# Four small edits to a fused attention and MLP kernel: the first load in two transfers, a longer row of constant products, another order of the three products of the second layer, and the weighted values at the end of a step

## The chip, the cores and the metric

The kernel runs on one core of one Trainium2 chip. The metric is the device time of one launch in microseconds (us); smaller is better. The core's engines are TensorE (PE in the rows, its weight loads PEld), VectorE (DVE), ScalarE (ACT), GpSimd (POOL) and SyncE (SP, which here issues nearly all DMA transfers). Each engine works through its own queue in order.

## The reference

Banded attention with a few global columns, then an MLP over all tokens:

```
q, k, v: (4, 8, 768, 64) fp32; n_global = 8; n_local = 96
scores = q k^T / 8 - slope_h * distance, kept where column < n_global or 0 <= row - column < n_local
a = softmax(scores);  attn = a v                       -> x, (3072, 512)
h = x @ w_in          (512 -> 2048)
g = h * clip(h + 3, 0, 6) / 6
out = g @ w_out       (2048 -> 512), fp32
```

The weights arrive as 64-bit words and are decoded to fp32 on the chip.

## The kernel before, in words

Tokens are worked in 8 blocks of 384 (two for each of 4 batch elements). A block's attention has 4 pairs of heads. The first three blocks (pairs 0 to 11) are attended ahead of everything else, in the loop of `banded` over `n` from -2 to 12; the later blocks' attention is woven into the MLP of the block before them (`attention`). The weights are decoded on DVE, ACT and POOL in between (`decode`, four steps for each of 32 chunks), at a pace that `work` sets from given costs.

Step `n` of the early loop does, in program order: the distances of pair n+2 (`distances`, ACT and POOL, n up to 1); `scores(t)` of pair n+2 for its three row tiles (PE, line 773); then for t = 0, 1, 2: `weigh` of pair n+2 (DVE line 788 adds the distances and takes the row's least value, ACT line 792 takes the exponential and the sums), `turn(t)` of pair n (PE transposes, lines 818 and 820, copied out by ACT or, for t = 1, DVE, line 822), and at t = 0 `sum_up` (DVE lines 800 and 801), at t = 1 `normalize` (POOL line 810) of pair n+1. `values` of pair n-1 stands at t = 1: PE products (line 862) into the only bank of the pool `xp`, then `put_x`: `xh` by ACT (line 152) and `xl` by DVE (line 153). It ends with the load of later values on SP. While `self.more` holds (n up to 7) the banks of the MLP serve as score banks and no half of the MLP is worked; from n = 8 the halves of the first MLP block go in between.

The order of PE, SP and POOL is the program's, pinned by `in_order`. The order on DVE and ACT is chosen by the framework's scheduler when the kernel is built.

At the start `banded_setup` issues `iv` (four integers, broadcast to 128 partitions) on ACT's queue and the loads of pairs 0 and 1 on SP's (`load`, line 289: 504 columns of keys and 384 of queries, 888 fp32 columns in one transfer). The masks are built from `iv`, from them `distances`, and the first `weigh` needs these. `wake` (line 353) issues seven products of a constant on PE, each two instructions, ahead of the first scores.

The MLP works in units of f (16 for each block): `first` (12 products of 384 columns, line 166), `gate` and the split of the gate's result into a high part `gh` (ACT or POOL) and a low part `gl` (DVE line 191, from `gh`), and `second` (line 198), nine products of 512 columns: for each of three row tiles gh x w2h, gl x w2h, gh x w2l. `second` of one f stands behind `first` of the next.

Of the kernel before, what the change touches and what calls it, by code (L numbers as in the profile page):

```python
# [21 lines left out]
TB = NT * P  # L22
# [10 lines left out]
KW = PREV + NT * TG  # L33
QW = 2 * TB
VW = 2 * NT * P
LOAD = KW + QW + VW
# [8 lines left out]
BOTH = 10  # L45
ROOMS = 2
MORE = 3
LEAD = 6
WAKE = 7
FIRST = 6  # L50

def store(nc, pool, out, row, acc, last=False):
# [6 lines left out]
class Kernel:  # L59
# [134 lines left out]
    def second(self, f, acc, gh, gl):  # L194
        for tt in range(NT):
            tk = slice(tt * P, (tt + 1) * P)
            for j, (a, w) in enumerate(((gh, self.w2h), (gl, self.w2h), (gh, self.w2l))):
                self.nc.tensor.matmul(acc[tt], lhsT=a[:, tk], rhs=self.w2(w, f),  # L198
                                      start=(f == 0 and j == 0), stop=(f == NF - 1 and j == 2))

# [84 lines left out]
    def load(self, n, values):  # L285

        if n < len(self.blocks) * NPAIR:
            columns = slice(KW + QW, LOAD) if values else slice(0, KW + (TB if n < BOTH else QW))
            self.nc.sync.dma_start(out=self.place(n)[:, columns], in_=self.pairs[n, :, columns])

    def load_next(self, n, values):

# [55 lines left out]
    def wake(self):  # L348

        any_ = self.three.broadcast_to([P, P])  # L350
        out = self.ps_x.tile([P, BANK], F32, name="xp")[:, 0:P]
        for _ in range(WAKE):
            self.nc.tensor.matmul(out, lhsT=any_, rhs=any_, start=True, stop=True)
# [99 lines left out]
    def banded(self, flag):  # L453

        self.banded_setup()
        start = len(self.nc.cur_bb.bb.instructions)
        self.common(2, 2)
        self.ps_s = self.pool("ps_s", 1, PSUM)
        self.ps_t = self.pool("ps_t", 1, PSUM)
        self.ps_x = self.pool("ps_x", 1, PSUM)  # L460
        self.turn, self.more, self.score_banks = {}, True, 1
        self.wake()
        self.raw, self.z, self.e, self.given, self.decoded = {}, {}, {}, [0.0, 0.0], 0
        self.last, self.op = None, None
        self.weights()
        with ExitStack() as early, ExitStack() as words:
            x0 = self.x_tiles(self.pool("x0", 1, ctx=early, side="right"))
            xs = [x0, self.x_tiles(), self.x_tiles()]
            self.decoding(words, 2, 2, side="right")
            self.decoding_steps = self.decode()  # L470

            def decoded_all():
                words.close()
                self.op = self.pool("op", 2, ctx=early, side="right")

            self.decoded_all = decoded_all
            self.fetch(0)
            self.given[1] = LEAD
            self.allowed = 4 * NF + 3
            acc = []  # L480
            with ExitStack() as ctx:
                self.room += self.rooms(self.pool("more", 1, ctx=ctx), MORE - ROOMS, ROOMS)
                self.load(2, False)
                self.fetch(1)
                for n in range(ROOMS):
                    self.load(n, True)
                self.plain_distances(ctx)
                self.attending(ctx, 0, 9, 5)
                pairs = [Pair(self, n, xs[n // NPAIR], True) for n in range(EARLY)]
                todo = self.halves([(0, f, xs[0], acc) for f in range(FIRST)])  # L490

                def half():
                    if not self.more:
                        next(todo, None)

                for n in range(-2, EARLY + 1):
                    if n + 2 < NPAIR:
                        self.distances(n + 2)
                    if n == 8:
                        self.more = False  # L500
                        acc.extend(self.acc_tiles())
                    if n + 2 < BOTH:
                        weigh = [pairs[n + 2].scores(t) for t in range(NT)]
                        self.load_next(n + 2, False)
                        self.work(1.440, 0)
                    for t in range(NT):
                        if n + 2 < EARLY:
                            if n + 2 < BOTH:
                                weigh[t]()
                            else:  # L510
                                pairs[n + 2].scores(t)()
                                if t == NT - 1:
                                    self.load_next(n + 2, False)
                            self.work(0 if n + 2 < BOTH else 0.78, 0.64)
                            if t == NT - 1 and n == -2:
                                self.load(2, True)
                        if 0 <= n < EARLY:
                            pairs[n].turn(t)
                            self.work(0.396, 0)
                        if n + 1 in (0, 1):  # L520
                            pairs[n + 1].sum_up(t)
                            pairs[n + 1].normalize(t)
                        if t == 0:
                            if 2 <= n + 1 < EARLY:
                                pairs[n + 1].sum_up()
                            half()
                        if t == 1:
                            if n > 0:
                                pairs[n - 1].values()
                                self.work(1.350, 0.47)  # L530
                            if 2 <= n + 1 < EARLY:
                                for u in range(NT):
                                    pairs[n + 1].normalize(u)
                        if t == 2:
                            half()
                for _ in todo:
                    pass
            self.weights()
            self.allowed = 4 * (2 * NF + 1)
            acc1 = [pool.tile([P, BANK], F32, name=name) for pool, name in ((self.ps_s, "sp"), (self.ps_t, "tp"), (self.ps_x, "xp"))]  # L540
            self.given[1] = max(self.given)
            todo = [(1, f, xs[1], acc1) for f in range(FIRST)]
            todo += [(i, f, xs[i], (acc, acc1)[i]) for f in range(FIRST, NF) for i in range(2)]
            for _ in self.halves(todo):
                pass
        self.attending(self.ctx, 2, 3, 2, side="right")
        self.bp = self.pool("bp", 2, side="right")
        self.there = self.pool("there", 2, bass.MemoryType.DRAM)
        self.score_banks = 2
        self.op = self.pool("op", 3, side="right")  # L550
        x, ahead = xs[2], None
        for i in range(2, len(self.blocks)):
            units, x_next = [], None
            if i + 1 < len(self.blocks):
                x_next = self.x_tiles()
                units, ahead = self.attention(i + 1, x_next, ahead)
                if i == 2:
                    units = [[]] + units
            else:
                units = [[]] * 4 + [[lambda: self.doubt(flag)]]  # L560
            acc = self.acc_tiles()
            for k, _ in enumerate(self.halves([(i, f, x, acc) for f in range(NF)], True)):
                for unit in units[k] if k < len(units) else ():
                    unit()
            x = x_next
        self.finish()
        self.in_order(start)
        return acc
# [373 lines left out]
```

## Time and profile before

| | |
|---|---|
| time, median of 3 runs | 672.31 us (672.19 to 672.88) |
| time of the profiled execution | 671.4 us |
| its span, first to last instruction | 669.6 us |
| busy share of the span | PE 98%, PEld 87%, DVE 63%, ACT 42%, POOL 33% |

The profile is of one execution. The 1.8 us between its time and its span lie around the program. Busy PE is not PE at its best rate, so the shares are read stage by stage.

### The profile page before, as it was taken

To read this page: it belongs to the slowest core of one execution; us is meant where nothing else is said; L and a number is where in the kernel's file an instruction comes from. 1 tells how busy PE (TensorE), PEld (TensorE's weight loads), DVE (VectorE), ACT (ScalarE), POOL (GpSimd) and SP (SyncE) were. 2 spreads that over 40 slices of the span, in tenths; PEclk is the share of its full clock that TensorE was granted. 3 is DMA by queue.
4 is the path that set the end of the run, shared out by engine and by line. 5 is a ranking of instruction groups with operands and counts; after the bars stand their busy time and mean duration, and the time that the engine had idled before them with its cause. 6 is when DMAs were issued, how large, how long until landed. Compare 5 with 4: busy or idle time off the path is not lost.

```text
span 669.6 us, 11375 instructions
## 1 busy us (share of the span) xinstructions
PE 654.7 (98%) x3919; PEld 584.1 (87%) x3919; DVE 424.3 (63%) x1121; ACT 278.4 (42%) x736; POOL 217.9 (33%) x389
## 2 busy tenths in 40 slices
PE   7989999999999999999999999999999999999996
PEld 5768789888999999999999989899999999989995
DVE  6799999999235776366663876457662777422221
ACT  6798755655235333153424433143331444121111
POOL 3766621221000553133340444225340444312110
PEclk9999999999999999999999999999999999999999
DMA  8577544442004366625663366524554256510001
GB/s 294 147 233 238 176 155 150 129 155 95 1 0 134 95 173 180 181 75 135 165 163 125 88 170 185 151 83 127 147 161 134 79 150 145 139 48 1 1 1 52
DMA packets 60692, 84.73 MB, mean 127 GB/s; under 512 B 8400, under 2 KB 45264, under 8 KB 60624
## 3 DMA queue, kind: packets, MB, share of 16 engines
q1 hardware_dynamic: 60336, 83.64, 43.3%
q8 instruction: 33, 0.54, 0.3%
q14 instruction: 35, 0.29, 0.1%
q10 hardware_dynamic: 288, 0.26, 0.1%
HBM read 62.92 MB, written 20.97 MB: 125 GB/s over the span
## 4 chain that ended last, share of the span: by engine, by line
PE 81%; DVE 7%; ACT 4%; DMA 3%; POOL 2%; issue 2%; POOLq 0%; ACTq 0%; SPq 0%; DVEq 0%
PE hp L166 36%; PE acc L198 33%; ACT n L792 3%; DMA wst<-w 2%; PE sp L777 2%; PE xp L862 2%; PE tp L862 2%; PE tp L777 2%; POOL n L810 1%; DVE wz L394 1%; DVE wz L400 1%; PE sp L198 1%; PE tp L198 1%; PE xp L198 1%; DVE wz L385 1%
## 5 line engine op out<-in xcount | busy, mean ns | idle before, releaser
L177 ACT ACTIVATE g<-hp,small 128x384 f32<-128x384 f32 x127 | 73.7, 580 | 254.2 <-PE hp L166 227.5
L166 PE MATMUL hp<-xh,w1h 128*128 128x384 f32 x512 | 174.0, 340 | 0.3 <-ACT w1h L404 0.3
L166 PE MATMUL hp<-xh,w1l 128*128 128x384 f32 x512 | 172.9, 338 | 0.1
L166 PE MATMUL hp<-xl,w1h 128*128 128x384 f32 x512 | 171.9, 336 | 0.0
L184 POOL TENSOR_SCALAR gh<-g 128x384 fp32r<-128x384 f32 x96 | 51.5, 537 | 294.0 <-DVE g L178 276.8
L198 PE MATMUL acc<-w2h,gl 128*128 128x512 f32 x336 | 133.1, 396 | 0.1
L198 PE MATMUL acc<-w2l,gh 128*128 128x512 f32 x336 | 132.7, 395 | 0.0
L198 PE MATMUL acc<-w2h,gh 128*128 128x512 f32 x336 | 132.2, 393 | 0.0
L178 DVE SCALAR_TENSOR_TENSOR g<-g,hp 128x384 f32<-128x384 f32 x128 | 69.7, 545 | 86.6 <-ACT g L177 86.0
L810 POOL TENSOR_SCALAR n<-n,sums 128x232 f32<-128x232 f32 (+1 forms) x186 | 102.0, 564 | 36.6 <-DVE sums L801 17.5
L191 DVE TENSOR_TENSOR gl<-g,gh 128x384 fp32r<-128x384 f32 x128 | 79.4, 621 | 50.4 <-POOL gh L184 45.4
L792 ACT ACTIVATE n<-n,least 128x232 f32<-128x232 f32 (+1 forms) x192 | 89.0, 465 | 45.7 <-DVE least L788 44.3
L166 PEld LDWEIGHTS hp<-xh,w1h 128*128 128x128 f32 x512 | 96.3, 188 | 5.9 <-issue 1.4
L166 PEld LDWEIGHTS hp<-xl,w1h 128*128 128x128 f32 x512 | 96.2, 188 | 3.8
L166 PEld LDWEIGHTS hp<-xh,w1l 128*128 128x128 f32 x512 | 96.0, 188 | 0.4 <-DVE w1l L391 0.4
L198 PEld LDWEIGHTS acc<-w2l,gh 128*128 128x128 f32 x336 | 63.0, 188 | 13.2
L198 PEld LDWEIGHTS acc<-w2h,gl 128*128 128x128 f32 x336 | 63.2, 188 | 12.4 <-DVE gl L191 1.7
L198 PEld LDWEIGHTS acc<-w2h,gh 128*128 128x128 f32 x336 | 63.3, 188 | 10.6 <-POOL gh L184 0.3
L835 DVE STREAM_TRANSPOSE blocks<-n 128x256 f32<-128x256 f32 x112 | 43.5, 424 | 29.2 <-POOL n L810 18.7
L367 POOL TENSOR_SCALAR we<-wst 128x512 int32<-128x512 uint32 x32 | 25.5, 797 | 70.3 <-DMA wst<-w 63.2
L748 POOL TENSOR_SCALAR kx<-load 64x504 fp32r<-64x504 f32 (+1 forms) x40 | 31.1, 778 | 37.8 <-PE hp L166 36.2
L788 DVE CUSTOM_DVE_ANT_0 n<-sp,d 128x232 f32<-128x232 f32 (+1 forms) x70 | 23.7, 375 | 30.9 <-PE sp L777 30.6
(110 smaller groups left out, 780.7 us busy)
## 6 DMA issues: line engine op xcount, KB each, us to landing
wst<-w SPq DMA_DIRECT2D x32, 512.0 KB, 3.5
load<-pairs SPq DMA_DIRECT2D x22, 636.0 KB, 5.2
there<-blocks SPq DMA_DIRECT2D x52, 256.0 KB, 2.6
load<-pairs SPq DMA_DIRECT2D x32, 384.0 KB, 4.0
weights<-there SPq DMA_DIRECT2D x48, 192.0 KB, 4.1
out<-o SPq DMA_DIRECT2D x23, 256.0 KB, 2.2
weights<-there SPq DMA_DIRECT2D x32, 160.0 KB, 3.2
load<-pairs SPq DMA_DIRECT2D x10, 444.0 KB, 4.0
```

The costliest lines, as they stand in the source:

```text
L166: self.nc.tensor.matmul(hp, lhsT=self.w1(w, f)[:, kt, :], rhs=a[:, kt, :], start=(n == 0), stop=(n == 3 * NKT - 1))
L177: nc.scalar.activation(out=g, in_=hp, func=AF.Relu, bias=self.three, scale=1.0)
L178: nc.vector.scalar_tensor_tensor(out=g, in0=g, scalar=6.0, in1=hp, op0=ALU.min, op1=ALU.mult)
L184: self.nc.gpsimd.tensor_scalar(out=gh, in0=g, scalar1=1.0, scalar2=0.0, op0=ALU.mult, op1=ALU.add)
L191: self.nc.vector.tensor_tensor(out=gl, in0=g, in1=gh.bitcast(F32), op=ALU.subtract)
L198: self.nc.tensor.matmul(acc[tt], lhsT=a[:, tk], rhs=self.w2(w, f), start=(f == 0 and j == 0), stop=(f == NF - 1 and j == 2))
L748: nc.gpsimd.tensor_scalar(out=part["kx"][own, c], in0=k[own, c], scalar1=1.0, scalar2=0.0, op0=ALU.mult, op1=ALU.add)
L777: nc.tensor.matmul(sp[j][:, lo:W], lhsT=q[:, t], rhs=part["kx"][:, c], start=(m == 0), stop=(m == 1))
L792: nc.scalar.activation(out=e[:, j, lo:W], in_=e[:, j, lo:W], func=AF.Exp, bias=self.least[:, i:i + 1], scale=-1.0, accum_out=self.sums[:, ...
L810: nc.gpsimd.tensor_scalar(out=e[:, j, lo:W], in0=e[:, j, lo:W], scalar1=over, scalar2=0.0, op0=ALU.mult, op1=ALU.add)
L835: nc.vector.transpose(out=blocks[:, :, s].rearrange("p b j q -> p j b q"), in_=e[:, :, c:c + P].rearrange("p j (b q) -> p j b q", b=4))
L862: nc.tensor.matmul(xps[j * D:(j + 1) * D, t * P:(t + 1) * P], lhsT=vt[0:K, t, j * D:(j + 1) * D], rhs=self.part(t, j, c, K), start=(c == 0 ...
```

## The change

Four edits. `load` of pair 0's keys and queries becomes two transfers (keys, then queries). `wake` issues nine products and not seven. In `second` the product with `gl` is the last of each three. In the early loop, for n = 1 to 7, `values` of pair n-1 and the `work` call behind it move from t = 1 (ahead of `normalize` of pair n+1, and of `weigh` and `turn` of t = 2) to t = 2, behind `turn(2)` and so straight ahead of the next step's scores; from n = 8 they stay where they were.

```diff
-WAKE = 7
+WAKE = 9
...
-            for j, (a, w) in enumerate(((gh, self.w2h), (gl, self.w2h), (gh, self.w2l))):
+            for j, (a, w) in enumerate(((gh, self.w2h), (gh, self.w2l), (gl, self.w2h))):
...
-            columns = slice(KW + QW, LOAD) if values else slice(0, KW + (TB if n < BOTH else QW))
-            self.nc.sync.dma_start(out=self.place(n)[:, columns], in_=self.pairs[n, :, columns])
+            end = KW + (TB if n < BOTH else QW)
+            for columns in (slice(KW + QW, LOAD),) if values else (slice(0, KW), slice(KW, end)) if n == 0 else (slice(0, end),):
+                self.nc.sync.dma_start(out=self.place(n)[:, columns], in_=self.pairs[n, :, columns])
...
                         if t == 1:
-                            if n > 0:
+                            if n > 0 and not self.more:
                                 pairs[n - 1].values()
                                 self.work(1.350, 0.47)
                             if 2 <= n + 1 < EARLY:
                                 for u in range(NT):
                                     pairs[n + 1].normalize(u)
                         if t == 2:
+                            if n > 0 and self.more:
+                                pairs[n - 1].values()
+                                self.work(1.350, 0.47)
                             half()
```

## Rows read from the trace of the kernel before

**Rows 1.** Busy time by stretch: PE, PEld, DVE, ACT, POOL, granted clock, DMA share, GB/s.

```profile
10.00:15.00 5.00, 4.37 (x19) 2.74 (x15) 5.00 (x33) 5.00 (x23) 0.00 (x0) 1.00 0.96 352
...
20.00:30.00 10.00, 9.39 (x94) 7.31 (x94) 7.09 (x33) 8.04 (x30) 7.12 (x19) 1.00 0.69 176
...
120.00:170.00 50.00, 49.77 (x247) 44.25 (x247) 47.53 (x88) 27.76 (x48) 9.15 (x12) 1.00 0.36 117
170.00:270.00 100.00, 100.00 (x556) 90.78 (x556) 56.68 (x146) 37.64 (x97) 26.36 (x47) 1.00 0.36 103
```

**Rows 2.** The chain of waits, shares of the span by engine.

```profile
PE 81%; DVE 7%; ACT 4%; DMA 3%; POOL 2%; issue 2%; POOLq 0%; ACTq 0%; SPq 0%; DVEq 0%
```

**Rows 3.** The chain in order of time, first 18 us: start, us, what.

```profile
0.73 4.32 DMA iv<-bounds
...
6.83 0.60 ACT p L317 x2
...
9.32 2.65 ACT n L792 x12
...
17.29 1.20 POOL n L810 x2
```

**Rows 4.** DMA issues at 0.7 us, and the stores of the run: us to landing.

```profile
load<-pairs SPq DMA_DIRECT2D x1, 444.0 KB, 4.1
iv<-bounds ACTq DMA_DIRECT2D x1, 2.0 KB, 4.3
...
out<-o SPq DMA_DIRECT2D x23, 256.0 KB, 2.2
```

**Rows 5.** Timeline, start: start, us, instruction, [idle before <- what ended it].

```profile
0.92 3.36 PE L353 MATMUL xp<-small 128*128 128x128 f32 x14 [0.92 <-DVE small L103]
...
4.93 0.58 PE L773 MATMUL sp<-load 64*128 64x128 f32 x1 [0.65 <-DMA load<-pairs]
...
7.45 0.29 DVE L788 CUSTOM_DVE_ANT_0 n<-sp,p 128x128 f32<-128x128 f32 x1 [0.72 <-ACT p L317]
```

**Rows 6.** PE's transposes by line, 5 to 20 us, then 21 to 50 us.

```profile
L818 PE MATMUL hp<-ident,n 128*128 128x128 f32 x4 | 1.8, 448 | 1.2 <-DVE n L808 1.2
...
L818 PE MATMUL hp<-ident,n 128*128 128x128 f32 x25 | 6.5, 286 | 0.0
```

**Rows 7.** Timeline of one early step, 25 to 32 us.

```profile
25.07 2.47 POOL L810 TENSOR_SCALAR n<-n,sums 128x128 f32<-128x128 f32 x6 [0.44 <-DVE sums L801]
...
28.96 0.17 DVE L800 TENSOR_SCALAR sums<-sums 128x6 f32<-128x6 f32 x1 [1.14 <-ACT n L792]
...
29.32 0.56 DVE L153 TENSOR_TENSOR xl<-xp,xh 128x384 fp32r<-128x384 f32 x1
...
29.94 1.32 PE L862 MATMUL xp<-pt,load 128*64 128x128 f32 x20 [0.49 <-DVE xl L153]
...
30.23 0.49 ACT L792 ACTIVATE n<-n,least 128x232 f32<-128x232 f32 x1 [0.46 <-DVE least L788]
...
31.19 0.33 PE L818 MATMUL hp<-ident,n 128*128 128x128 f32 x1
```

**Rows 8.** Waits of ACT, 20 to 50 us: total, times, longest.

```profile
ACT n L792 <- DVE least L788: 3.9, 4, 2.5
```

**Rows 9.** Timeline: a low part awaited at 156 us, and the last unit.

```profile
156.24 0.19 PEld L198 LDWEIGHTS sp<-w2h,gl 128*128 128x128 f32 x1 [0.32 <-DVE gl L191]
...
661.72 0.56 DVE L191 TENSOR_TENSOR gl<-g,gh 128x384 fp32r<-128x384 f32 x1 [0.73 <-POOL gh L184]
661.74 0.51 PE L198 MATMUL acc<-w2h,gh 128*128 128x512 f32 x1
...
662.34 0.50 PE L198 MATMUL acc<-w2h,gl 128*128 128x512 f32 x1
...
662.90 0.39 PE L198 MATMUL acc<-w2h,gh 128*128 128x512 f32 x1
663.13 0.39 PE L198 MATMUL acc<-w2h,gl 128*128 128x512 f32 x1
```

## Prediction

> **What bounds the kernel now.** I read the table by stretch first. At 170 to 270 us PE is busy for all of the 100 us, and before that, at 120 to 170 us, it has 49.77 of 50 while DVE has 47.53 of 50 [rows 1]. The reader is to see two regimes: a long end that only PE sets, and a beginning in which PE is never what is short. There, at 10 to 15 us, ACT and DVE are both busy for all of the 5 us, and at 20 to 30 us the busiest engine is idle in name only: PE shows 9.39 of 10, but with small products, and ACT 8.04 [rows 1]. The chain of waits agrees: 81% of the span is PE, and the rest is the early DVE, ACT, DMA and POOL work [rows 2]. Followed in order of time, the chain starts at none of the big loads: it starts with `iv`, a transfer of 2 KB that takes 4.32 us, goes through the masks to ACT's distances at 6.83 us, runs through ACT's exponentials and reaches POOL's normalization at 17.29 us [rows 3]. PE has no part in these 17 us. So three things can move the end: the head of that chain, the ACT and DVE work of the early steps (a us won there is a us at the end, as every queue behind it moves along in its fixed order), and PE's own idle time behind.
>
> **The first load in two.** The load removed lands 4.1 us after its issue at 0.73 us, at 4.83 us; the first score product starts at 4.93 us and ends at 5.51 us [rows 3 to 5]. The DVE instruction that reads it starts at 7.45 us and waited for ACT's distances, not for PE [rows 5]. The scores have 7.45 - 5.51 = 1.94 us to spare, so earlier keys are worth nothing by themselves, and a second issue on SP, which moves every later load of the beginning back by one issue, is covered by the same 1.94 us for pair 0. What is not covered is `iv`. Its 2 KB need 4.3 us, while a store of 256 KB needs 2.2 us [rows 4]: 2.1 us of it are, by the nearest row, time beside the loads. A row of the load is 888 x 4 = 3,552 bytes and becomes 2,016, then 1,536. If the pieces of `iv` take turns with rows of the load, the 2.1 us shrink by at most 1 - 2016/3552 = 43%, or 0.9 us. At the other end nothing changes, or one more transfer stands in the way; I set that end at 0.4 us lost. As pair 1's load follows with whole rows, I take a third of the 0.9: **0.3 us won**, at the head of the chain, so in full.
>
> **Nine products for seven.** Fourteen instructions take 3.36 us, 0.24 each [rows 5]. Four more run from about 4.28 to 5.24 us and so push the first score product from 4.93 to 5.24 us at most: 0.3 of the 1.94 us to spare. Cost **0**, cover the wait for the distances; it would cost from 1.94 us on. PE then has no gap from 0.92 us through the first scores. [...]
>
> **The low part last.** In the last unit DVE starts `gl` at 661.72 us, PE's first product runs at 661.74, and the second, which needs `gl`, starts at 662.34; later ones follow each other every 0.23 us (662.90, 663.13) [rows 9]. With the product of `gh` and `w2l` second, two of the nine are issued before `gl` comes and seven, not eight, behind it: **0.23 us won**, with the store behind it moving along. The same at 156 us, where the weight load waited 0.32 us for `gl` [rows 9]: what follows is one product shorter, 0.23 us. In the stage with PE at 100% [rows 1] `gl` is early and nothing changes. The other end is that `w2l`, the last result of a chunk's decoding, is now needed 0.23 us sooner; no row shows a wait for it, so I set the loss between 0 and 0.23 and take 0. Together **0.46 us**.
>
> **The weighted values at a step's end.** For seven steps, 20 or 24 PE products, ACT's `xh`, DVE's `xl`, a load on SP and the decode steps that `work` draws move behind `normalize`, `weigh` and `turn` of t = 2. What stands ahead of the next scores on PE is the same work in both orders, the values and four transposes; only their order differs. The values wait for the `xl` before (0.49 us at 29.94), and the transposes of `turn(2)` stand behind them at 31.19 us, though POOL had finished their input at 27.54 us [rows 7]. Turned round, the transposes fill that wait, and the values have their `xl` long before. SP's load of later values is issued perhaps 1.3 us later, one length of the values [rows 7], for a pair used three steps on; a fetch of weights queued behind it would be as late, but `work` stays behind `values`, so it isn't queued differently. PE is not the bound here, though: DVE waited 1.14 us for ACT's last exponential, then did the sums and `xl`, and only then `weigh`, for which ACT waited 0.46 us [rows 7]. Such waits are 3.9 us in four times; the longest, 2.5 us, I put to the distances at the beginning, which leaves **1.4 us** in three [rows 8]. That is the most that this edit can win directly. It wins it if `xl` (0.56 us) comes out from between the sums and `weigh`. But DVE's and ACT's order is set by the scheduler from the changed program, and it may as well put `xl` where it waits longer: seven steps with another 0.46 us each lose **3.2 us**. I take half of the gain, **0.7 us**, since PE's wait for `xl` goes in any case and nothing new stands ahead of `weigh`.
>
> **The sum.** 0.3 + 0 + 0.46 + 0.7 = 1.46 us. Against the profiled execution, 671.4 us for a span of 669.6, that is 669.9; the median shown is 0.9 us above that execution, so 672.31 - 1.46 = 670.85, say **670.8 us**. 0.2%, or 1.34 us, is about what a measurement of this kernel can tell from no change; the forecast is only just beyond it.
>
> **Rivals.** *Only the ends pay*: the scheduler leaves DVE and ACT as they were, the freed PE time is idle time, and 0.3 + 0.46 remain: 671.5 us. For it: PE isn't on the early chain [rows 3]. Against: the 1.4 us of [rows 8] lie behind an instruction that moves. *The moved `xl` holds `weigh`*: 672.31 - 0.76 + 3.2 = 674.7 us, slower. It decides once a step's added wait exceeds 0.76/7 = 0.11 us. For it: `xh` now comes a step's end later, right when `weigh` of the next pair is due; against: PE has the values' inputs earlier. *The second transfer lands late*: if the queries came a whole landing time (4.1 us) after the first part, 4.1 - 1.94 = 2.2 us are lost, and 672.31 - 0.46 - 0.7 + 2.2 = 673.3 us. Against it: both parts are on the same queue, one issue apart. [...]
>
> **How the numbers follow.** Forecast 0.45, only the ends 0.31, `xl` holds `weigh` 0.16, second transfer late 0.03, clock pays 0.05. Faster by over 0.2%: 0.45 + 0.05 = 0.50. Within: 0.31 + 0.03 = 0.34. Slower: 0.16. The likeliest case's own range is 669.5 to 671.0. The range reaches from all gains at their bounds, 672.31 - 0.9 - 0.46 - 1.4 - 0.65 = 668.9, to the late second transfer, 673.4; it leaves out the slower case and a little below, under 0.2.
>
> **What would show it.** Right: `iv` lands before 5.05 us and `weigh` starts before 7.45; the last unit issues two products ahead of the wait for `gl`; ACT's waits for the least values at 25 to 50 us shrink and everything behind 50 us stands over 1 us earlier. Wrong: `iv` as late as before, or `weigh` waiting for PE; exponentials further apart than before; a wait for `w2l`; or a fetch of weights that comes later and holds the decoding, so that a gain at 50 us is gone at 170.

## The result, and the profile after

The changed kernel takes 673.5 us in the median of 20 executions (671.2 to 676.5), the kernel before beside it 672.0 (20 executions, 671.4 to 673.1). The ratio is 1.0023, 95% interval 1.0013 to 1.0034: 1.5 us slower, where 1.5 us faster was forecast, and just above the range. The profiled execution of the changed kernel, 672.37 us for a span of 670.6, is one of its shorter ones, so the trace shows less of the loss than the median does.

In the changed file the lines have moved: the load is L290, the constant's products L354, scores L777, `weigh` L792, the exponentials L796, the sums L804, `turn` L822 and L824, its copies L826, the values L866.

The start first: the timeline of after, then the chain of waits in order of time, then the DMA issues at 0.7 us.

```profile
0.92 4.21 PE L354 MATMUL xp<-small 128*128 128x128 f32 x18 [0.92 <-DVE small L103]
...
5.06 0.58 PE L777 MATMUL sp<-load 64*128 64x128 f32 x1
...
5.82 0.80 ACT L318 ACTIVATE p<-d 128x232 f32<-128x232 f32 x3 [3.15 <-POOL d L276]
...
6.59 0.29 DVE L792 CUSTOM_DVE_ANT_0 n<-sp,p 128x128 f32<-128x128 f32 x1 [0.87 <-PE acc L777]
```

```profile
0.92 4.21 PE xp L354 x18
...
16.24 0.60 POOL n L814 x2
```

```profile
load<-pairs SPq DMA_DIRECT2D x1, 252.0 KB, 3.1
iv<-bounds ACTq DMA_DIRECT2D x1, 2.0 KB, 3.3
```

`iv` now needs 3.3 us where it needed 4.3 [rows 4], ACT's distances start 1.01 us earlier and POOL's normalization 1.05 us earlier [rows 3]. DVE's first `weigh` starts 0.86 us earlier than in [rows 5], and what ends its wait is new: PE's scores, not the distances. The chain of waits now starts with the products of the constant and no longer with `iv`.

The table by stretch, columns as in [rows 1], with one stretch added at 44 to 47 us:

```profile
10.00:15.00 5.00, 3.08 (x17) 1.96 (x16) 5.00 (x33) 5.00 (x23) 0.00 (x0) 0.80 1.02 383
...
20.00:30.00 10.00, 8.96 (x95) 7.13 (x94) 7.08 (x33) 8.04 (x30) 6.84 (x18) 1.00 0.71 202
...
44.00:47.00 3.00, 3.00 (x16) 2.35 (x15) 2.70 (x15) 2.78 (x11) 2.15 (x5) 0.50 0.71 159
...
120.00:170.00 50.00, 49.87 (x248) 44.29 (x247) 48.66 (x91) 28.63 (x50) 9.99 (x13) 1.00 0.39 127
170.00:270.00 100.00, 100.00 (x557) 90.89 (x556) 56.12 (x144) 38.22 (x97) 26.36 (x47) 1.00 0.35 99
```

The chain of waits, shares of the span by engine, has hardly changed against [rows 2]; a loss of 0.2% doesn't show there:

```profile
PE 81%; DVE 7%; DMA 4%; ACT 3%; issue 3%; POOL 1%; SPq 0%; ACTq 0%; POOLq 0%; DVEq 0%
```

In the table the late stretches are as before. At 20 to 30 us PE is busy 8.96 where it was 9.39 [rows 1], and at 44 to 47 us, where the kernel before has 1.00, the granted clock is 0.50: PE is busy for all of the 3 us and gets 16 matmuls done. The line of the kernel before for the same 3 us:

```profile
44.00:47.00 3.00, 2.58 (x34) 2.00 (x34) 2.97 (x17) 2.59 (x10) 2.57 (x6) 1.00 0.79 240
```

PE's transposes, at 5 to 20 and at 21 to 50 us, answer to [rows 6]:

```profile
L822 PE MATMUL hp<-ident,n 128*128 128x128 f32 x6 | 2.4, 405 | 1.8 <-DVE n L812 1.8
...
L822 PE MATMUL hp<-ident,n 128*128 128x128 f32 x20 | 5.1, 287 | 1.1 <-ACT pt L826 1.0
```

At the start the clock column of after reads 0.80 at 10 to 15 us and 0.52 at 15 to 20; its transposes take 0.42 to 0.47 us from 14.38 to 16.49 us, where it reads 0.50, and 0.27 from 20.03 us on, where it reads 1.00. The column of before reads 1.00 throughout the first 20 us, yet its transposes take 0.42 to 0.47 us from 15.43 to 17.54 us and 0.27 at 20.62, 448 and 286 ns in the means of [rows 6]: at the start the column of before can't be relied on.

One early step of after, on all engines, in order of time; it answers to [rows 7]:

```profile
28.24 0.57 ACT L826 COPY pt<-hp 128x512 f32<-128x512 f32 x1
...
28.37 0.17 DVE L804 TENSOR_SCALAR sums<-sums 128x6 f32<-128x6 f32 x1 [1.14 <-ACT n L796]
...
28.71 0.48 ACT L152 CAST xh<-xp 128x384 fp32r<-128x384 f32 x1
...
29.22 0.56 DVE L153 TENSOR_TENSOR xl<-xp,xh 128x384 fp32r<-128x384 f32 x1 [0.45 <-ACT xh L152]
...
29.83 1.32 PE L866 MATMUL xp<-pt,load 128*64 128x128 f32 x20 [0.25 <-DVE xl L153]
...
30.12 0.49 ACT L796 ACTIVATE n<-n,least 128x232 f32<-128x232 f32 x1 [0.94 <-DVE least L792]
...
31.08 0.46 PE L777 MATMUL sp<-load 64*128 64x232 f32 x1
```

Read it from ACT. Its copy of the turned weights (`pt`, 28.24) now stands ahead of `xh` (28.71). In the kernel before, `xh` came first and `pt` behind it:

```profile
28.84 0.46 ACT L152 CAST xh<-xp 128x384 fp32r<-128x384 f32 x1
...
29.20 0.58 ACT L822 COPY pt<-hp 128x512 f32<-128x512 f32 x1
```

`xl` on DVE needs `xh`, so DVE, done with the sums, waits 0.45 us, a wait that the trace of before does not have. `weigh` stands behind `xl` on DVE, and ACT waits for `weigh` 0.94 us instead of the 0.46 of [rows 7]. The copy's 0.47 us thus go once round ACT, DVE and ACT again. Scores start at 21.92, 26.03, 31.08, 36.07 and 43.52 us; in the kernel before at 22.99, 27.20, 31.77, 36.33 and 42.09. Steps of 4.6 us became steps of 5.0, and what the head had won, 1.07 us, is 0.26 by the fourth of these and a loss of 1.43 by the fifth.

That fifth step, in the timeline of after, PE and DVE:

```profile
39.51 0.27 PE L824 MATMUL hp<-ident,n 128*128 128x128 f32 x1
...
41.39 0.55 DVE L153 TENSOR_TENSOR xl<-xp,xh 128x384 fp32r<-128x384 f32 x1
...
42.05 1.54 PE L866 MATMUL xp<-pt,load 128*64 128x128 f32 x24 [2.26 <-issue]
43.52 0.45 PE L777 MATMUL sp<-load 64*128 64x128 f32 x1
```

Here DVE does four of the next pair's `weigh` and a piece of the decoding ahead of `xl`, PE's values need `xl` and have nothing else ahead of them, and PE is idle for 2.26 us. The profile names no releaser ("issue"), but the values start as `xl` ends. Within 2 us of its end stand the 3 us at half pace.

The waits of after between 20 and 60 us, in total, times and longest:

```profile
ACT n L796 <- DVE least L792: 5.4, 4, 2.5
...
PE xp L866 <- issue: 2.3, 1, 2.3
...
DVE xl L153 <- ACT xh L152: 1.2, 3, 0.4
```

The first line reads the same between 20 and 50 us alone, and so answers to [rows 8], 3.9 us there.

Last, PE in the last unit, which answers to [rows 9]:

```profile
662.71 0.51 PE L198 MATMUL acc<-w2h,gh 128*128 128x512 f32 x1
...
663.05 0.40 PE L198 MATMUL acc<-w2l,gh 128*128 128x512 f32 x1
...
663.30 0.50 PE L198 MATMUL acc<-w2h,gl 128*128 128x512 f32 x1
...
664.81 0.40 PE L198 MATMUL acc<-w2h,gl 128*128 128x512 f32 x1
```

Two products run ahead of the one that needs `gl`. From the first start to the last it is 2.10 us; before it was 2.29, 661.74 to 664.03.

### The profile page after: what moved, and what is told of

It reads as the page before. It is cut to its first block, busy times and chain, and to the rows that moved or that the text cites. A ratio compares the mean times of both kernels' runs of the same rounds, so it can differ in the third digit from the quotient of the medians.

```text
span 670.6 us, 11432 instructions
## 1 busy us (share of the span) xinstructions
PE 653.6 (97%) x3923; PEld 584.2 (87%) x3923; DVE 423.8 (63%) x1121; ACT 279.4 (42%) x736; POOL 218.6 (33%) x389
## 4 chain that ended last, share of the span: by engine, by line
PE 81%; DVE 7%; DMA 4%; ACT 3%; issue 3%; POOL 1%; SPq 0%; ACTq 0%; POOLq 0%; DVEq 0%
PE hp L166 35%; PE acc L198 32%; DMA wst<-w 4%; PE xp L866 3%; PE sp L781 2%; PE tp L866 2%; PE tp L781 2%; ACT n L796 2%; DVE wz L395 1%; POOL n L814 1%; DVE n L792 1%; DVE wz L386 1%; PE sp L198 1%; PE sp L777 1%; DVE gl L191 1%
## 5 line engine op out<-in xcount | busy, mean ns | idle before, releaser
L796 ACT ACTIVATE n<-n,least 128x232 f32<-128x232 f32 (+1 forms) x192 | 89.2, 467 | 47.0 <-DVE least L792 46.2
L792 DVE CUSTOM_DVE_ANT_0 n<-sp,d 128x232 f32<-128x232 f32 (+1 forms) x70 | 23.6, 374 | 30.2 <-PE sp L781 29.9
```

The costliest lines, as they stand in the source:

```text
L792: nc.vector.tensor_tensor_reduce(out=e[:, j, lo:W], in0=sp[j][:, lo:W], in1=d, op0=ALU.add, op1=ALU.min, scale=scale, scalar=3.0e38, accum ...
L796: nc.scalar.activation(out=e[:, j, lo:W], in_=e[:, j, lo:W], func=AF.Exp, bias=self.least[:, i:i + 1], scale=-1.0, accum_out=self.sums[:, ...
```

## The experiments

Two theories stood at first for the loss. **A**: moving the values costs, through the late `xl` (A2) or through SP's fetch of weights, which comes at 49.82 us instead of 46.83, behind the later load of values (A1). **C**, the author's guess of a cause: PE's clock, which the nine products bring up earlier and which then falls again. The ratios below are all against the kernel before, run on the same chip.

### Each part alone, and all but the move

Four kernels hold one part of the change each.

> The kernel before with the first load in two transfers alone. Theory A (the head is won, the moved weighted values lose more): the four integers land about 1.0 us earlier than in the kernel before, at 4.1 us and not 5.08, and as nothing behind is late the time falls by the same, to 671.0 us. Rival B (the landing of a small transfer beside big ones is chance, the 1.0 us seen was luck): no change, 672.0 us within 0.4.

> The kernel before with nine products of a constant alone. Theory A: PE is not on the chain there, 672.0 us within 0.4. Rival C (the longer row lets TensorE's clock rise early, and it then falls at gaps of PE later on, and this is what makes the changed kernel slow and its times spread over 5 us): slower by 1 us or more, times spread as in the changed kernel, and stretches at half the granted clock between 10 and 50 us in the profile.

> The kernel before with the low part's product last alone. By the prediction's term 0.46 us are won, 671.55 us: in the last unit two products are issued before the low part comes and seven behind it. Rival: a wait for the low part of the decoded weights takes it back, 672.0 us.

> The kernel before with the weighted values at the step's end alone. Theory A: the fetch of the fifth weight chunk stands on SP behind a load that waits for the values, is issued about 3 us later, and the decoding behind it starts 2 us later: 674.0 to 675.0 us. Rival C (clock): without the longer row of products the clock does not come into it, 672.0 us within 0.5.

| alone | median, us | before, us | ratio | 95% interval |
|---|---|---|---|---|
| load in two | 671.10 | 671.92 | 0.9984 | 0.9974 to 0.9993 |
| nine products | 672.03 | 671.92 | 0.9996 | 0.9988 to 1.0005 |
| low part last | 670.82 | 671.92 | 0.9979 | 0.9970 to 0.9988 |
| values moved | 674.74 | 671.92 | 1.0042 | 1.0025 to 1.0058 |

The first three are won 0.8, 0 and 1.1 us; the move alone loses 2.8. Then the three without the move, the values where they were:

> The changed kernel with the weighted values back at t = 1: the first load in two, nine products and the low part last remain. Theory A (the move alone loses): the gains of the single edits add, 0.8 us for the load, 1.1 for the low part, 0 for the nine products, so 670.0 us, faster than both kernels. Rival C (nine products and a clock that falls again spoil it): above 671 us, with times spread over several us.

It takes 670.31 us against 671.99, ratio 0.9973 (0.9962 to 0.9985). The 1.7 us won are the sum of the parts within their intervals. The move alone turns it into a loss: the change stands 1.0023 - 0.9973 = 0.5%, 3.4 us, above this kernel. Theory C, as a cause by itself, falls: the nine products alone cost nothing (ratio 0.9996), and in their profile the granted clock reads 0.50 over 10 to 20 us and 1.00 over 40 to 50.

### The fetch of weights behind the load

```diff
...
+                            while late:
+                                self.load_next(late.pop(), True)
...
-                                pairs[n - 1].values()
+                                pairs[n - 1].values(load=False)
                                 self.work(1.350, 0.47)
+                                late.append(n - 1)
...
```

The load of later values is issued a step later, behind the fetch.

> The changed kernel with the load on SP that ends the moved values issued a step later (at t = 1 of the next step), so that the fetch of weights no longer stands behind it; PE, DVE and ACT keep the moved values. Theory A1 (the fetch behind the load is the loss): the fourth fetch is issued at 44 us or earlier, not at 49.8, ACT's wait for the chunk at 55 us goes, and 1.5 to 2 us come back: 671.7 us. Rival A2 (the loss is that PE gets the values, and so the next scores, late, because DVE's low part of the values before stands behind weigh): the fetch is early and the time stays above 673 us.

673.70 us, ratio 1.0024 (1.0014 to 1.0034). The fetch came at 46.73 us, later than expected but as early as before, and nothing was won. A1 falls, unless this kernel loses elsewhere what it wins there; the pair of kernels below is to tell.

### `xl` pinned ahead of `weigh` on DVE, with and without the later load

```diff
+        self.xl = nc.cur_bb.bb.instructions[-1].name
...
+            if kk.more and kk.xl and t == 0 and j == 0:
+                kk.behind.append((nc.cur_bb.bb.instructions[at], kk.xl))
...
+        for i, name in self.behind:
+            self.tc.add_manual_dep(i, name, mybir.DependencyInfo(mybir.DependencyClass.NoSync, mybir.DependencyReason.DATA), reason="xl first")
```

> The changed kernel with one order more on DVE: the low part of a pair's values always stands ahead of the next pair's weigh, as in the kernel before. Theory A2 (the late low part is the cause): PE's gap of 2.3 us at 40 us goes, and with it the fall of the clock at 44 to 47 us; scores and the fetch behind them come 1.2 us or more earlier, 671.5 to 672.3 us. Theory A1 (only the fetch counts): the fetch still waits for the values at the step's end and is 1.5 us late, 673 us or more.

672.54 us, ratio 1.0003 (0.9994 to 1.0012). PE's idle time is 1.36 us in place of 2.26, the clock stays at 1.00, and some 1.3 us come back: part of the loss, not all. That left open whether the fetch had been hidden behind the later `xl` only, so both together:

> The changed kernel with DVE's xl ahead of the next pair's weigh, and SP's load of later values a step later, so that the fetch of weights isn't behind it. If the fetch that came 3 us late was hidden only by the later xl, it shows here: 671 us, over 1 us under the kernel with xl first alone. If the fetch matters in neither: 672.5 us.

672.21 us, ratio 1.0003 (0.9994 to 1.0012): the fetch, at 45.61 us here, matters in neither.

### The values behind `weigh(2)`, but still ahead of `turn(2)`

```diff
+                        if t == 2 and n > 0 and self.more:
+                            pairs[n - 1].values()
+                            self.work(1.350, 0.47)
                         if 0 <= n < EARLY:
                             pairs[n].turn(t)
...
```

> The changed kernel with the values moved only half the way: behind weigh of t = 2, but ahead of turn(2), so that PE's and SP's orders are those of the kernel before and only the priorities for DVE and ACT follow the move. If PE's place of the values is the cause, it is as fast as without the move, 670.0 us. If the order that the scheduler then gives DVE and ACT is the cause, it is as slow as the changed kernel, 673 us or more.

670.91 us, ratio 0.9983 (0.9973 to 0.9992). Moved past `weigh` and `normalize`, but not past `turn`, the values cost nothing that shows. What the move must not pass is `turn(2)`. By the expectation that speaks for PE's place of the values; but in this trace `xh` (27.66 us) also stands ahead of ACT's copy (28.02) again, so PE's order and ACT's are still to be told apart.

### `xh` pinned ahead of that copy on ACT

PE's order stays the change's own; only ACT's copy of `turn(2)` is tied behind `xh`.

```diff
+        self.xh = nc.cur_bb.bb.instructions[-1].name
...
-                            pairs[n].turn(t)
+                            copy = pairs[n].turn(t, t == 2 and n > 0 and self.more)
...
                                 pairs[n - 1].values()
+                                at = len(self.nc.cur_bb.bb.instructions)
+                                copy()
+                                self.behind.append((self.nc.cur_bb.bb.instructions[at], self.xh))
...
```

> The changed kernel with one thing pinned: on ACT the copy of the weights turned for t = 2 stands behind the xh of the pair before, as it did in the kernel before; PE's order stays that of the change. Theory A2 (the late xl, brought by ACT's copy that now stands ahead of xh, stretches the steps and opens PE's gap of 2.3 us at 40 to 42 us): steps are back near 4.5 us, scores of the fifth pair start by 36 us, the granted clock does not fall at 44 to 47 us, and the time is 670.3 to 671.2 us. Rival (PE's own order is what costs: the values right ahead of the scores make the scores late, whatever ACT does): steps stay near 5 us and the time stays at 672.5 us or more.

670.77 us against 672.27, ratio 0.9982 (0.9973 to 0.9991). The same step in its timeline:

```profile
27.70 0.45 ACT L152 CAST xh<-xp 128x384 fp32r<-128x384 f32 x1
...
28.06 0.58 ACT L834 COPY pt<-hp 128x512 f32<-128x512 f32 x1
28.19 0.56 DVE L154 TENSOR_TENSOR xl<-xp,xh 128x384 fp32r<-128x384 f32 x1
...
29.10 0.49 ACT L803 ACTIVATE n<-n,least 128x232 f32<-128x232 f32 x1 [0.46 <-DVE least L799]
...
29.29 1.32 PE L874 MATMUL xp<-pt,load 128*64 128x128 f32 x20
...
30.54 0.46 PE L784 MATMUL sp<-load 64*128 64x232 f32 x1
```

`xl` follows DVE's sums without a wait, ACT's wait is back at 0.46, PE's values wait for nothing, and the scores start at 26.04, 30.54, 35.05 and 41.17 us: steps of 4.50, 4.51 and 6.12 us, where the kernel without the move has 4.57, 4.51 and 5.77. At 40 to 50 us the clock reads 1.00. That settles A2: with PE's order of the change and, on ACT, the order of before for these two instructions, the loss is gone. And the move has won nothing either: the kernel without it stands at 0.9973, within the interval.

### Filling PE's idle time

Is the half pace at 44 to 47 us part of the loss, or only seen beside it? A first kernel does the transposes of the sixth pair's `turn(2)` five times over:

```diff
-                            pairs[n].turn(t)
+                            pairs[n].turn(t, 5 if (n, t) == (5, 2) else 1)
...
-        for j in range(2):
+        for j in [0, 1] * times:
```

> The changed kernel with the two transposes of turn(2) of the sixth pair done five times over, in PE's idle time at 40 to 42 us; the extra ones write the same results again. If the fall of the granted clock to 0.50 at 44 to 47 us comes from that idle time, it is gone here. If those 3 us at half pace are on the path to the end: 672.5 us or less, about 1 us under the changed kernel. Rival (PE catches up there anyway, and the loss is the stretched steps alone): 673.5 us, with the clock up or not.

672.14 us, ratio 1.0000 (0.9991 to 1.0009), the clock at 1.00 at 44 to 47 us. But DVE and ACT had also been given another order behind 45 us, so that doesn't tell the clock from the order. A second kernel puts sixteen transposes into the finished instruction list, so that the other four engines' orders are the change's own, instruction by instruction:

```diff
+            for _ in range(times):
+                nc.tensor.transpose(old.outs[0].bass_ap, old.ins[1].bass_ap, old.ins[0].bass_ap)
...
+            bb.instructions = rows[:at] + new + rows[at:]
```

> The changed kernel, with a transpose of turn(2) of the sixth pair issued sixteen more times by PE in its idle time at 40 to 42 us, and every instruction of the other engines in the same order as in the changed kernel (the earlier kernel that fills this time also had another order on DVE and ACT behind 45 us). If the half pace at 44 to 47 us costs what that earlier kernel won: clock at its full level there and 672.0 to 672.5 us, ratio about 1.000. If the half pace costs nothing and the other order won: clock at its full level, and 673.4 us or more, ratio about 1.0023.

> The changed kernel itself, beside the run above on the same chip: 673.5 us, ratio 1.0023 as before, if its time does not hang on the chip.

On one chip, against 671.83 us before: filled 672.00 us (671.2 to 673.5), ratio 1.0004 (0.9995 to 1.0013); the change itself 674.50 (672.1 to 676.6), 1.0047 (1.0033 to 1.0060). Work that computes nothing new, put where PE was idle, wins 2.5 us. The filled kernel's timeline of PE, and its table at 44 to 47 us:

```profile
39.97 1.91 PE L943 MATMUL hp<-ident,n 128*128 128x128 f32 x16
41.72 0.27 PE L824 MATMUL hp<-ident,n 128*128 128x128 f32 x1
41.83 0.27 PE L826 MATMUL hp<-ident,n 128*128 128x128 f32 x1
42.60 0.66 PE L870 MATMUL xp<-pt,load 128*64 128x128 f32 x8 [0.50 <-PE hp L826]
```

```profile
44.00:47.00 3.00, 3.00 (x31) 2.47 (x30) 2.62 (x13) 2.48 (x8) 1.58 (x4) 1.00 0.66 167
```

31 matmuls in the 3 us, not 16. The long step stays long, 7.43 us from scores to scores where the change has 7.45, so filling does not win by shortening it. Beside it the change itself, in this second profile of it, the same two views:

```profile
42.56 1.54 PE L866 MATMUL xp<-pt,load 128*64 128x128 f32 x24 [2.25 <-issue]
```

```profile
44.00:47.00 3.00, 3.00 (x32) 2.50 (x32) 2.61 (x13) 2.65 (x10) 1.62 (x4) 1.00 0.68 163
```

The same idle time, 2.25 us, and this time no fall of the clock; that execution took 672.14 us, the shortest of its five. So the idle time doesn't bring the fall each time. It does in two more kernels with the move, in which PE is idle for 2.25 us there. First the move alone (its profiled execution took 674.74 us; PE starts again at 43.06), then the later load (673.61 us; 41.74):

```profile
44.00:47.00 3.00, 3.00 (x25) 2.16 (x21) 2.19 (x9) 2.09 (x9) 1.45 (x4) 0.58 0.54 151
```

```profile
44.00:47.00 3.00, 3.00 (x20) 2.34 (x18) 2.83 (x15) 2.46 (x9) 2.45 (x6) 0.61 0.21 24
```

The move alone has seven products of a constant, so the fall doesn't need the nine.

The times point the same way: of the change's 25 executions, the 12 whose mean granted clock over the span is 0.988 or less take 674.8 us on average (672.5 to 676.6), the other 13 take 672.8 (671.2 to 674.6); the filled kernel's mean clock was never below 0.990. This is a hint and no more, since the mean also counts the first 20 us (in profiles, 0.66 over 10 to 20 us for the change, 0.50 for the nine products alone): with the nine products alone, three executions at 0.988 or less took 671.3 to 672.1 us, no longer than the others. No execution of the change above 672.4 us was profiled, so where the longer ones lose their time is not shown.

### The best version

The load in two and the low part last, seven products of a constant, values where they were:

> The load in two and the low part last, with seven products of a constant and the values where they were. If the two parts that won alone (0.8 and 1.1 us) add up and the nine products do nothing: 670.0 to 670.4 us, level with the kernel that has all but the move. If the nine products help once the load is in two (PE without a gap ahead of the first scores): 670.8 us or more.

669.65 us against 672.27, ratio 0.9964 (0.9951 to 0.9977, from 5 executions): by the ratio 2.4 us faster than the kernel before. It is level with the one that has the nine products too (0.9973), within the intervals.

## Why the prediction was wrong, step by step

**The values at a step's end: the step that failed.** The text said: "I take half of the gain, **0.7 us**, since PE's wait for `xl` goes in any case and nothing new stands ahead of `weigh`." Both reasons were false. PE still waited for `xl`, 0.25 us at 29.83 us and 2.26 us at 42.05. And something new did stand ahead of `weigh`, at one remove: the copy of `turn(2)` ahead of `xh` on ACT, `xh` ahead of `xl`, `xl` ahead of `weigh`. In the long step DVE had them the other way about, `xl` behind four of `weigh`, and there PE waited. The prediction followed the moved instructions on PE, SP and DVE, and asked of the scheduler only where it would put `xl`; it had `xh` come later in a rival, but nowhere set it against the copy. On ACT these two instructions, whose own time the edit doesn't change, had changed places, because in the program the values had moved past the `turn` that issues the copy. In place of 0.7 won, the move lost 2.8 us alone and 3.4 on top of the rest.

The rival *The moved `xl` holds `weigh`* was what happened. Its price, 0.46 us a step, is what two steps show (5.05 and 4.99 us where the kernel without the move has 4.57 and 4.51). Its count, seven such steps, was not: the rest came in one step with decoding in it (7.45 us against 5.77), and in what filling PE's idle time brings back. Its point of decision, 0.11 us a step, was passed fourfold.

**How the loss divides.** Filled, the change stands at 1.0004, so 1.0004 - 0.9973 = 0.0031, 2.1 us, is what filling does not bring back. The stretched steps are of that size: by the fifth scores the change is 43.52 - 41.55 = 1.97 us behind the kernel without the move. The rest, 1.0023 or 1.0047 less 1.0004, is 1.3 to 2.9 us that filling brings back. That all of it is half pace is argued and not shown. The two profiles of the change, with the fall and without it, differ by less: from the fifth scores to the first store 162.03 us (43.52 to 205.55) against 160.85 (44.03 to 204.88), 1.2 us, and to the store at 599 us only 0.5 us. Where the rest of it lies, in executions that were not profiled, stays open. The prediction had the clock only as a gain. What decides between the fall to 0.50 in one profile of the change and the 1.00 behind the same idle time in the other is not shown.

**The first load in two: right in kind, too small.** The 0.3 us were a third of the 0.9 that the shorter rows could give; measured are 0.8 (0.5 to 1.7). Even the whole bound was a little low: `iv` came 1.0 us earlier. It needs 3.2 to 3.5 us in all twelve profiles with the load in two, and 4.3 in all four with the load whole. Pair 1's load behind it, for which I took two thirds off, did not take them. That pieces of `iv` take turns with rows of the load is not shown by this; the runs show only that it lands earlier. The rival of a second transfer that lands late falls: the scores start at 5.06 us. In this trace the first part lands sooner, in 3.1 us where the whole load took 4.1, but what won is `iv`.

**Nine products: right at 0 alone, but not beside the load in two.** The 1.94 us to spare were counted up to distances that the first edit then brings 1.0 us earlier, and from the end of the first score product, while the profile has `weigh` wait for a later one. Where the distances hold the first `weigh`, it starts 0.62 to 0.63 us behind ACT's start on them ([rows 3] and [rows 5]; 5.94 and 6.57 us with seven products and the load in two). In the change it waits for PE, and the chain of waits starts with the constant's products; `weigh` starts 0.77 us behind (5.82 and 6.59), in the second profile of the change 0.99 (5.78 and 6.77): 0.1 to 0.4 us of the head are lost again. That is too little to show in the times of the best version. The range of the prediction also counts 0.65 us for the clock, and its chances 0.05: no run shows that term. With nine products alone the time is 672.03 us against 671.92, and in that profile transposes still take 0.42 us at 21.10 us, where those of before take 0.27 from 20.62 us on.

**The low part last: right in kind, too small.** 0.46 was forecast, 1.1 measured (0.8 to 2.0). "In the stage with PE at 100% [rows 1] `gl` is early and nothing changes" failed. The waits of PE's weight loads tell, behind 170 us, in the kernel before (total, times, longest):

```profile
PEld acc L198 <- DVE gl L191: 1.5, 5, 0.4
```

and in the one with the low part last:

```profile
PEld acc L198 <- DVE gl L191: 0.8, 3, 0.3
```

Five waits, of which I had seen one, the last. The first, 0.29 us at 202.53 us, lies inside the very stretch that reads 100.00 of 100 [rows 1]: the column of PE's products doesn't show a wait of its weight loads. Between 60 and 170 us there are five more, 1.5 us in all, of which I had counted one; with the low part last there are three, 1.2 us. In that kernel the first store is issued 0.5 us earlier than before, the one at 598 us 1.0.

**The fetch of weights.** "It isn't queued differently" was wrong: it came 3 us later. It cost nothing, as the later load showed.

## What to carry to other kernels

When a group of instructions is moved past another, list what each engine's queue gets in a new order, also for instructions whose own time does not change; the one that hurt here, a copy of 0.5 us on ACT, sits on an engine whose order the prediction did not follow. Where the engines of a loop wait for each other in turn, as ACT, DVE and ACT do here, such a delay can be lost again step by step: 0.48 us in each of two steps. And an idle time of PE ahead of a busy stretch can have a cost behind it (2.25 to 2.26 us of it stood ahead of a granted clock of 0.50 to 0.61 over 3 us in three profiles here, and of 1.00 in a fourth): look at the granted clock there, and time several executions before trusting one profile.

## What the runs showed of the hardware

- The granted clock fell, to a mean of 0.50, 0.58 and 0.61 over 44 to 47 us, within 2 us after an idle time of PE of 2.25 to 2.26 us with small products on either side, in the profiles of three kernels with the move, and read 1.00 in another execution of one of them with an idle time of 2.25 us. In the change's own profile transposes took 0.42 us at 46.57 us, at a clock of 0.50, and 0.27 at 47.27. With the idle time filled it stayed at 1.00 in the profiles of two kernels, and of the one that keeps the other engines' orders the time is 672.0 us where the change takes 674.5; how much of that is the clock's is not shown.
- A transfer of 2 KB beside the first load landed in 3.2 to 3.5 us (twelve profiles) instead of 4.3 (four) when that load was cut into two: 0.8 to 1.1 us of its time hung on how the load beside it was cut.
- In the changed kernel transposes take 0.42 to 0.47 us where the granted clock reads 0.50 (14.38 to 16.49 us) and 0.27 where it reads 1.00 (from 20.03 us). In the kernel before it reads 1.00 over the first 20 us, while transposes take 0.42 to 0.47 us at 15.43 to 17.54 us and 0.27 at 20.62 us (448 and 286 ns in the means): at the start it can't be relied on.
